# A fused attention and gated-MLP kernel on one Trainium2 core: the scores of attention tile 4 are written behind the outputs of tile 2 instead of in front of them

## The chip, the core and the metric

The kernel runs on one core of a Trainium2 chip. The core has a matrix engine (TensorE, PE in the profile, with its weight loads as PEld), a vector engine (VectorE, DVE), an activation engine (ScalarE, ACT), a general-purpose engine (GpSimd, POOL) and a synchronisation engine (SyncE, SP), which here issues all DMAs. Each engine works through its own list of instructions in order and waits for the others at semaphores. The metric is the time of one execution on the device, in microseconds (us).

## The reference

The program computes block attention over chunks of 64 tokens, and feeds the result into a gated MLP that also mixes along the sequence. Sizes: B = 8 batches, H = 8 heads, S = 576 tokens, D = 64 per head, so the model width is 512; d_ff = 1024.

```python
scores = scale * q_c @ k_c.T                 # per chunk of 64 tokens
attn   = softmax(scores)                     # minus the row maximum, / (sum + 1e-09)
x      = attn @ v_c                          # -> (B, S, 512)

h    = gelu_tanh(x @ w_in)                   # (B, S, 1024)
u, v = h[..., :512], h[..., 512:]
v_n  = (v - mean(v)) / sqrt(var(v) + 1e-06) * g_ln
v_s  = einsum('ts,bsd->btd', w_sg, v_n) + b_sg[None, :, None]
out  = x + (u * v_s) @ w_out
```

All inputs and outputs are float32; in memory w_in and w_out arrive as 8-byte words, which the kernel turns into float32 pairs itself.

## The kernel before, in words

**Tiles and units.** The 8 x 576 tokens make 36 attention tiles of 128 tokens (tile 4 has the last 64 tokens of batch 0 and the first 64 of batch 1). For each tile there are three steps: `S` (scores and softmax, `att_scores`), `T` (transpose of the probabilities, `att_transpose`) and `O` (outputs, `att_out`). An output tile is evacuated by `keep()` into three copies: `xh` (the high part, cast on ScalarE, L94), `xl` (the rest, subtracted on VectorE, L97) and `xf` (the full value, copied on ScalarE, L432). The MLP of a batch is made of units: five or four `v` units (x @ the v half of w_in for 128 tokens, gelu, layer norm), four `u` units (x @ a quarter of the u half, gelu), four `s` units (w_sg @ v_n, gate) and four `o` units (@ w_out, plus x, store). The name v02 is the unit v of batch 0, part 2; v04 is the fifth part, which takes the odd 64 tokens of batches 0 and 1 together. Products of high precision are made of three matmuls each (high x high, high x low, low x high).

**The weights.** w_in has to be split into a high and a low part. `W`/`w` do it for the v half (four pieces), `X`/`x` for the u half (four pieces): `X` (`pair_begin`, L130 on ScalarE, then L131, L132, L133, L162, L166 on VectorE) prepares the words in place, and `x` (`pair_end`) forms the high part on ScalarE (L174), sums four products on TensorE (L178) in a PSUM buffer, and evacuates the low part on ScalarE (L179). `G` issues the loads of w_sg (L235) and its bias, `g` splits one of its five pieces each (L94 or L250 on ScalarE, L97 or L251 on VectorE). `L` and `A` issue loads of w_in and of the attention inputs (L297, L301), `M` a small load, `D` some spare matmuls; `P`, `Q` are scores and outputs of two tiles at once, `Y` prepares w_out.

**A v unit.** Twelve matmuls (L452) into a PSUM buffer; gelu on ScalarE (L455, output `hs`); L458, L459, L460 on VectorE take mean and variance (`sm`); GpSimd raises the variance to the power -0.5 (L461); L467 on VectorE subtracts the mean and multiplies by g_ln; L469 on ScalarE and L470 on VectorE write the high and the low part. In v04, L474 and L475 on ScalarE (two each) and L476 on VectorE take the place of the last two, and write `z`. A u unit is 24 matmuls and one gelu on ScalarE (L496).

**Buffers.** There are three PSUM buffers `pm` in rotation: for scores, for L178's products, and for the v, u, s and o units. The next user of a buffer waits until the evacuation of the one before is done. The transposes and outputs of tiles 0 to 4 alternate between two halves of one PSUM tile, `banks`: the transposes of tile 3 write where O2's outputs stood, so they wait for xh, xl and xf of tile 2; likewise tile 4's for tile 3's.

**Softmax.** For tiles 0, 2 and 4 (`ACT_SOFTMAX`) the exponentials are taken head by head on ScalarE (L344, eight instructions per tile) straight from the scores; in the others VectorE subtracts the maximum first (L346) and ScalarE takes one exponential (L349).

**What sets the order.** For batches 0 and 1 the order of all steps is written out by hand in the string `START`, a letter and a number for each step; a loop calls the functions in this order. A layer below records the instructions and, when the program is built, sets their order on each engine from these calls and from what they depend on, so moving one step in `START` can move instructions of other steps too. From batch 2 on, a table of slots places the attention steps between the units.

The lines that carry the name of a step in `START`:

```python
for step in START.split():
    steps[step[0]](int(step[1:]))
```

Of the kernel before, what the change touches and what calls it, by code (L numbers as in the profile page):

```python
# [42 lines left out]


START = """
L0 A0 L1 A1 L2 L3 A4 W0 S0 W1 D8 w0 S1 W2 T0 w1 S2 O0 T1 W3 w2 S3 O1 T2 M0 w3 S4 O2 T3 v00 X0 O3 G0 T4 v01 x0 X1 O4 A8
v02 x1 X2 v03 X3 v04 u00 x2 g0 g1 u01 x3 g2 P5 g3 u02 g4 T5 u03 T6 s00 P7 Q5 s01 s02 T7 T8 s03 Q7 v10 v11 Y0 v12 Y1
v13 Y2 u10 Y3 u11 Y4 u12 Y5 Y6 u13 Y7 A10 s10 A12 s11 P9 s12 s13 T9 o00 T10 P11 o01 o02 o03 Q9 A14 T11 o10 T12 o11 Q11
S13 A15 o12 T13 o13
# [587 lines left out]
```

## Time and profile before

| what | value |
| --- | --- |
| time, median of 3 runs (lowest to highest) | 508.56 us (508.21 to 508.85) |
| the profiled execution: time; span of its instructions | 508.83 us; 507.0 us |
| mean granted TensorE clock in it | 0.998 |
| busy share of TensorE, VectorE, ScalarE, GpSimd | 97%, 67%, 54%, 14% |

The time of an execution is a little longer than the span from the first to the last recorded instruction (here by 1.83 us). The busy share says in how much of the span an engine worked; all times of instructions below are counted from the start of the span. A row of a timeline gives start, duration, engine, line of the program, operation, output and inputs, sizes, how many instructions the row groups, and in brackets the idle time before it and what ended it. A row of the chain of waits gives start, length, engine, what it wrote, line.

### The profile page before, as it was taken

How to read it: one execution, taken by the hardware profiler on the slowest of the kernel's cores; microseconds unless marked ns; L12 is line 12 of the kernel's file. 1: busy time of each engine (PE TensorE's matmuls, PEld its weight loads, DVE VectorE, ACT ScalarE, POOL GpSimd, SP SyncE). 2: the span in 40 equal slices, each digit the busy share in tenths (PEclk: the TensorE clock that was granted, in tenths of full speed). 3: DMA queues.
4: the chain of work that ended last, by engine and by line, in shares of the span. 5: the costliest groups of instructions: out<-in, count | busy, mean ns of one | idle time of the engine just before them, and what ended most of it. 6: DMA issues, size and time to landing. Idle time of an engine off the chain costs nothing.

```text
span 507.0 us, 12386 instructions
## 1 busy us (share of the span) xinstructions
PE 494.4 (97%) x5244; PEld 458.1 (90%) x5244; DVE 339.1 (67%) x707; ACT 274.7 (54%) x509; POOL 69.9 (14%) x72
## 2 busy tenths in 40 slices
PE   5999999999999999999999999999999999999996
PEld 4667898799999899989999899999999899999996
DVE  7998779888856947586563866576565676536141
ACT  5899667753445764355642775355643766334210
POOL 0112100210211401022100321022100141002000
PEclk9999999999999999999999999999999999999999
DMA  8948010228167204241324204060415200010002
GB/s 335 326 136 234 3 35 25 69 78 207 34 186 227 64 11 117 86 134 39 89 66 154 63 1 127 37 183 2 125 26 170 87 1 4 25 71 0 1 1 93
DMA packets 49595, 46.58 MB, mean 92 GB/s; under 512 B 35202, under 2 KB 39554, under 8 KB 49540
## 3 DMA queue, kind: packets, MB, share of 16 engines
q1 hardware_dynamic: 49540, 45.80, 30.3%
q8 instruction: 41, 0.67, 0.6%
q14 instruction: 14, 0.11, 0.1%
HBM read 36.34 MB, written 9.44 MB: 90 GB/s over the span
## 4 chain that ended last, share of the span: by engine, by line
PE 88%; DVE 6%; ACT 4%; DMA 1%; issue 1%; POOL 0%; DVEq 0%; SPq 0%; ACTq 0%
PE pm L509 21%; PE pm L489 20%; PE pm L532 19%; PE pm L452 18%; PE banks L322 3%; PE pm L410 3%; PE pm L178 2%; ACT pt L344 1%; DMA qkv_t<-qkv 1%; PE pm L314 1%; PE pm L577 1%; DVE gl L97 1%; DVE gt L513 1%; ACT L455 1%; DVE blocks L372 1%
## 5 line engine op out<-in xcount | busy, mean ns | idle before, releaser
L509 PE MATMUL pm<-wsg,v 128*128 128x288 f32 x768 | 107.9, 296 | 0.0
L509 PEld LDWEIGHTS pm<-wsg,v 128*128 128x128 f32 x768 | 103.9, 189 | 0.3
L532 PE MATMUL pm<-gh,wout 128*128 128x288 f32 x512 | 92.3, 297 | 0.0
L532 PEld LDWEIGHTS pm<-gh,wout 128*128 128x128 f32 x512 | 76.1, 189 | 0.5
L461 POOL TENSOR_TENSOR sm<-sm,neg_half 128x1 f32<-128x1 f32 x36 | 36.5, 1013 | 165.6 <-DVE sm L460 165.6
L358 POOL TENSOR_TENSOR pt<-pt,den 128x512 f32<-128x512 f32 x27 | 29.7, 1113 | 202.4 <-DVE den L357 128.0
L94 ACT CAST gh<-gt 128x576 fp32r<-128x576 f32 x32 | 21.5, 673 | 63.2 <-DVE gt L513 63.2
L532 PE MATMUL pm<-gl,wout 128*128 128x288 f32 x256 | 55.4, 296 | 0.0
L489 PE MATMUL pm<-xh,win_l 128*128 128x288 f32 x256 | 55.3, 298 | 0.0
L489 PE MATMUL pm<-xh,win_h 128*128 128x288 f32 x256 | 55.0, 296 | 0.0
L489 PE MATMUL pm<-xl,win_h 128*128 128x288 f32 x256 | 55.0, 296 | 0.0
L452 PE MATMUL pm<-win_h,xl 128*128 128x512 f32 x128 | 51.5, 402 | 1.4 <-DVE xl L97 0.9
L452 PE MATMUL pm<-win_l,xh 128*128 128x512 f32 x128 | 50.8, 397 | 0.0
L452 PE MATMUL pm<-win_h,xh 128*128 128x512 f32 x128 | 50.8, 396 | 0.0
L513 DVE TENSOR_TENSOR gt<-pm,u 128x576 f32<-128x576 f32 x32 | 24.1, 754 | 38.9 <-PE pm L509 38.9
L540 DVE TENSOR_TENSOR ot<-pm,xf 128x576 f32<-128x576 f32 (+1 forms) x33 | 24.1, 733 | 29.8 <-PE pm L532 29.7
L489 PEld LDWEIGHTS pm<-xh,win_l 128*128 128x128 f32 x256 | 41.4, 188 | 1.0
L532 PEld LDWEIGHTS pm<-gl,wout 128*128 128x128 f32 x256 | 41.4, 189 | 0.0
L489 PEld LDWEIGHTS pm<-xl,win_h 128*128 128x128 f32 x256 | 41.1, 188 | 0.0
L489 PEld LDWEIGHTS pm<-xh,win_h 128*128 128x128 f32 x256 | 41.0, 188 | 0.0
L97 DVE TENSOR_TENSOR xl<-pm,xh 128x512 fp32r<-128x512 f32 (+1 forms) x34 | 21.8, 641 | 26.2 <-ACT xh L94 26.2
L458 DVE BATCH_NORM_STATS2 sm<-hs 128x6 f32<-128x512 f32 x36 | 24.8, 689 | 20.9 <-ACT hs L455 20.7
(121 smaller groups left out, 820.0 us busy)
## 6 DMA issues: line engine op xcount, KB each, us to landing
qkv_t<-qkv SPq DMA_DIRECT2D x32, 512.0 KB, 4.6
out_dram<-ot SPq DMA_DIRECT2D x31, 288.0 KB, 2.2
qkv_t<-qkv SPq DMA_DIRECT2D x124, 64.0 KB, 3.7
qkv_t<-qkv SPq DMA_DIRECT2D x3, 768.0 KB, 11.9
wsg<-w_in SPq DMA_DIRECT2D x4, 512.0 KB, 6.1
wout<-w_in SPq DMA_DIRECT2D x4, 512.0 KB, 4.2
st<-w_out SPq DMA_DIRECT2D x8, 256.0 KB, 2.7
stage<-w_sg SPq DMA_DIRECT2D x5, 288.0 KB, 4.0
```

The costliest lines, as they stand in the source:

```text
L94: nc.scalar.copy(hi, src)
L97: lo_eng.tensor_tensor(lo, src, hi.bitcast(F32), op=ALU.subtract)
L322: nc.tensor.matmul(sc[o, c, h // 2, :], qt[r, 0, h, :], qt[r, 1, h, :], start=True, stop=True)
L358: (nc.gpsimd if t > last[1] else pick(f"n{t}")).tensor_tensor(pt, pt, den.unsqueeze(2).broadcast_to([P, H, D]), op=ALU.mult)
L452: nc.tensor.matmul(pv, a[:, kt, tok], c[:, kt, DH:], start=(i == 0), stop=(i == 11))
L458: nc.vector.bn_stats(st, h)
L461: nc.gpsimd.tensor_tensor(rs, rs, neg_half, op=ALU.pow)
L489: nc.tensor.matmul(pm[:, j, :HS], a[:, kt, dc], c[:, kt, j * HS : (j + 1) * HS], start=(i == 0), stop=(i == 11))
L509: nc.tensor.matmul(pm[:, j, :HS], a[:, dc], c[:, m, j * HS : (j + 1) * HS], start=(i == 0), stop=(i == len(ops) - 1))
L513: nc.vector.tensor_tensor(gt.rearrange("p (a c) -> p a c", a=2), pm[:, :, :HS], u2[0][:, dt, :].rearrange("p (a c) -> p a c", a=2), op=ALU ...
L532: nc.tensor.matmul(pm[:, j, :HS], a[:, kt, ec], c[:, kt, j * HS : (j + 1) * HS], start=(i == 0), stop=(i == len(ops) - 1),)
L540: nc.vector.tensor_tensor(ot[:, js], pm[:, js, :HS], res[:, js], op=ALU.add)
```

## The change

The step `S4` moves behind the step `O2` in `START`; nothing else is edited.

```diff
 START = """
-L0 A0 L1 A1 L2 L3 A4 W0 S0 W1 D8 w0 S1 W2 T0 w1 S2 O0 T1 W3 w2 S3 O1 T2 M0 w3 S4 O2 T3 v00 X0 O3 G0 T4 v01 x0 X1 O4 A8
+L0 A0 L1 A1 L2 L3 A4 W0 S0 W1 D8 w0 S1 W2 T0 w1 S2 O0 T1 W3 w2 S3 O1 T2 M0 w3 O2 S4 T3 v00 X0 O3 G0 T4 v01 x0 X1 O4 A8
 v02 x1 X2 v03 X3 v04 u00 x2 g0 g1 u01 x3 g2 P5 g3 u02 g4 T5 u03 T6 s00 P7 Q5 s01 s02 T7 T8 s03 Q7 v10 v11 Y0 v12 Y1
```

No instruction is added or removed (ScalarE's list shows 3 rows more, because rows that were grouped fall apart). The order of S4's and O2's own matmuls on TensorE stays as it is; what changes on the engines behind it is this.

ScalarE, from tile 4's exponentials on (`pt`, `den` with L344; `xh` and `xf` are those of tile 2, `hs<-pm` is gelu of v00, then of v01; `ptT` is of tile 3, `win_h<-wsg_186` is x0's high part):

```order
-L344 ACTIVATE pt,den<-pm,nmax 128x64 x8
+L344 ACTIVATE pt,den<-pm,nmax 128x64 x2
 L94 CAST xh<-banks 128x2x4x64
-L455 ACT_TABLE_LOAD
-L455 ACTIVATE hs<-pm 128x512
+L344 ACTIVATE pt,den<-pm,nmax 128x64 x5
 L432 COPY xf<-banks 128x2x4x64
+L344 ACTIVATE pt,den<-pm,nmax 128x64
+L455 ACT_TABLE_LOAD
+L455 ACTIVATE hs<-pm 128x512
+L368 COPY ptT<-banks 128x512
 L174 ACTIVATE win_h<-wsg_186 128x4x128
```

Tile 2's cast xh moved from behind the eighth exponential to behind the second, its copy xf from behind the gelu of v00 to ahead of it and of the table load.

VectorE, between v00's L467 and the subtraction xl of tile 3, before (`wsg_234` are the words of x1's quarter, the first `v` is v00's low part, the L458 is v01's):

```order
L467 SCALAR_TENSOR_TENSOR hs<-hs,sm,g_bc 128x512
L131 TENSOR_SCALAR wsg_234<-wsg_234 128x512
L132 TENSOR_SCALAR wsg_234<-wsg_234 128x512
L133 SCALAR_TENSOR_TENSOR wsg_234<-wsg_234 128x512
L470 SCALAR_TENSOR_TENSOR v<-hs,sm,v 128x512
L458 BN_STATS sm<-hs 128x6
L97 TENSOR_TENSOR xl<-banks,xh 128x2x4x64
```

The same place now:

```order
L467 SCALAR_TENSOR_TENSOR hs<-hs,sm,g_bc 128x512
L458 BN_STATS sm<-hs 128x6
L131 TENSOR_SCALAR wsg_234<-wsg_234 128x512
L459 BN_AGGR sm<-sm 128x2
L132 TENSOR_SCALAR wsg_234<-wsg_234 128x512
L470 SCALAR_TENSOR_TENSOR v<-hs,sm,v 128x512
L97 TENSOR_TENSOR xl<-banks,xh 128x2x4x64
```

v01's statistics moved ahead of v00's low part, L133 behind xl.

ScalarE, from the last L469 of batch 0's v units to the gelus of u00 and u01 (`u_705`), before (`L179` is x2's low part, `bh` belongs to the bias of w_sg, the `z` are v04's):

```order
L469 ACTIVATE v<-hs,sm 128x512
L496 ACTIVATE u_705<-pm 128x576
L255 CAST bh<-bt 1x576
L179 ACTIVATE win_l<-pm 128x4x128
L474 ACTIVATE z_0_94<-hs,sm 64x512
L474 ACTIVATE z_1_95<-hs,sm 64x512
L475 CAST z_0_96<-z_0_94 64x512
L475 CAST z_1_97<-z_1_95 64x512
L496 ACTIVATE u_705<-pm 128x576
```

The same place now:

```order
L469 ACTIVATE v<-hs,sm 128x512
L255 CAST bh<-bt 1x576
L474 ACTIVATE z_0_94<-hs,sm 64x512
L474 ACTIVATE z_1_95<-hs,sm 64x512
L475 CAST z_0_96<-z_0_94 64x512
L475 CAST z_1_97<-z_1_95 64x512
L496 ACTIVATE u_705<-pm 128x576
L179 ACTIVATE win_l<-pm 128x4x128
L496 ACTIVATE u_705<-pm 128x576
```

The gelu of u00 and x2's L179 moved from ahead of v04's four z instructions to behind them.

Elsewhere: on TensorE the transposes of tile 3 come after two of v01's matmuls instead of seven, and those of tile 4 after four of v02's instead of five. On VectorE, between v02's L470 and v04's L460, the L162 and L166 of x3's quarter (`wout_376`) are now inside, and one L97 of w_sg and the L251 are behind; v02's L467 is followed by L133 instead of L166. SP issues w_sg's four loads (L235) ahead of tile 6's load (L297) instead of behind it. GpSimd's order is the same.

## The prediction

> **What bounds the kernel now.** I read the page first (busy shares), then TensorE's waits, then the chain of work that ended last, then the timelines of the engines that the chain names. The page says that TensorE is the bound:
>
> ```profile
> span 507.0 us, 12386 instructions
> PE 494.4 (97%) x5244; PEld 458.1 (90%) x5244; DVE 339.1 (67%) x707; ACT 274.7 (54%) x509; POOL 69.9 (14%) x72
> ```
>
> So a change of order can only add or take away moments in which TensorE waits. Its waits from 43 us to the end (what waited, for whom; us in total, times, longest) leave little:
>
> ```profile
> PE pm L410 <- ACT ptT L380: 0.9, 1, 0.9
> PE pm L452 <- ACT hs L455: 0.3, 1, 0.3
> ```
>
> What the change touches lies before 60 us. There the chain (start, length, what) leaves TensorE and comes back to it at 38.35:
>
> ```profile
> 28.21 2.48 ACT pt L344 x16
> 30.69 0.48 ACT xh L94
> ...
> 31.19 1.28 ACT L455
> ...
> 32.48 0.61 ACT hs L455
> 33.11 0.70 DVE sm L458
> ...
> 35.71 0.69 DVE wsg L133
> 36.40 0.66 DVE v L470
> 37.06 0.60 DVE sm L458
> 37.67 0.64 DVE xl L97
> ...
> 38.35 1.43 PE pm L452 x5
> ```
>
> The reader is to see: tile 4's eight exponentials, the cast xh of tile 2's outputs behind them, the table load for gelu, gelu of v00, its statistics on VectorE, and xl of tile 3, for which v02 waits. TensorE's timeline shows both waits, at v01 (31.95) and at v02 (38.35), and the later place x3 (58.13):
>
> ```profile
> 30.67 0.40 PE L452 MATMUL pm<-win_h,xh 128*128 128x512 f32 x1
> 31.95 0.50 PE L452 MATMUL pm<-win_h,xl 128*128 128x512 f32 x1 [0.88 <-DVE xl L97]
> 32.29 0.40 PE L452 MATMUL pm<-win_l,xh 128*128 128x512 f32 x1
> ...
> 37.66 0.59 PE L178 MATMUL pm<-win_h,ident 128*128 128x512 f32 x1
> 38.35 0.50 PE L452 MATMUL pm<-win_h,xl 128*128 128x512 f32 x1
> ...
> 58.13 1.02 PE L178 MATMUL pm<-wout,ident 128*128 128x512 f32 x2
> ```
>
> **Part 1: the wait at v01 goes.** No instruction is added or removed. S4's and O2's matmuls keep their places on TensorE; what moves is the evacuation of O2 on ScalarE and VectorE. The rows for it:
>
> ```profile
> 30.55 0.63 ACT L94 CAST xh<-banks 128x512 fp32r<-128x512 f32 x1
> 32.98 0.58 ACT L432 COPY xf<-banks 128x512 f32<-128x512 f32 x1
> 33.44 0.65 ACT L174 ACTIVATE win_h<-wsg 128x512 fp32r<-128x512 f32 x1
> 29.00 0.69 DVE L133 SCALAR_TENSOR_TENSOR wsg<-wsg 128x512 int32<-128x512 int32 x1
> 29.73 0.43 DVE L162 TENSOR_SCALAR wsg<-wsg 128x512 int32<-128x512 int32 x1
> ```
>
> xh of tile 2 now follows the second exponential, so at about 28.8 (28.21 plus two eighths of 2.48) instead of 30.55; it ends at 29.4. xl then stands on VectorE behind L133, which ends at 29.7, and is done by about 30.3. TensorE can use it when v00's last matmul (30.67) has gone: matmuls of this shape go in every 0.23 us (an estimate from 1.43 us for x5 less the last one's 0.5), so v01's second matmul moves from 32.29 to about 31.13. Gain 1.16 us. If the order brought nothing it would be 0; it cannot be more, since TensorE has no further idle time here.
>
> **Part 2: most of it comes back at v02.** ScalarE now does the copy xf (33.44 − 32.98 = 0.46 of its queue) ahead of the table load, so gelu of v00 starts at about 32.93 instead of 32.48, and the statistics and POOL's power follow 0.45 later. On VectorE v01's L458 moves ahead of v00's L470, and L133 of x1's quarter moves behind. L470 comes at about 36.6 (before: 36.32, queue-bound), xl of tile 3 directly behind it at 37.26 (before 37.60, with L458 between), v02 at 38.0 instead of 38.35. So of 1.16 us, 0.34 is left at v02, and TensorE waits there for about 1 us. The transposes of tile 4 then wait for xf of tile 3 about as in the kernel before; I carry 0.3 us of gain from v02 on. Ends: 0 to 0.6, by 0.2 to 0.3 us of ScalarE drain around the table load either way.
>
> The DMAs: w_sg's four loads wait on SP for O3, now at 35.4 instead of 36.56, and go ahead of tile 6's first load, which has until 59.7. ScalarE now casts the first of them at 39.0, before the copy ptT of tile 4 that O4 waits for. The time to landing of the first two:
>
> ```profile
> DMA to landing us min/median/max: 2.9/3.6/4.3
> ```
>
> With 2.9 it has landed at 38.3 and costs nothing; with 4.3 at 39.7 it would hold O4 by 0.7 us. The queues are empty in front of it as in the kernel before, so I take 2.9.
>
> **Part 3: a new wait at x3.** x3's first product (58.13) needs the PSUM buffer of u00, which gelu of u00 frees. In the kernel before, that gelu stands on ScalarE ahead of v04's four z instructions; now it stands behind them:
>
> ```profile
> 54.08 0.65 ACT L496 ACTIVATE u<-pm 128x576 f32<-128x576 f32 x1 [0.19 <-DVE wsg L97]
> 56.57 1.47 ACT L474 ACTIVATE z<-hs,sm 64x512 fp32r<-64x512 f32 x2 [0.52 <-POOL sm L461]
> 58.06 1.26 ACT L475 CAST z<-z 64x512 fp32r<-64x512 f32 x2
> 59.22 0.64 ACT L496 ACTIVATE u<-pm 128x576 f32<-128x576 f32 x1
> ```
>
> From the first z to the instruction behind the four are 59.22 − 56.57 = 2.65 us, plus 0.65 for the gelu itself. So x3 starts 3.35 us after z does (0.05 for the semaphore), and z starts when POOL's power of v04 is done. How early is that now? The rows:
>
> ```profile
> 38.67 0.74 DVE L467 SCALAR_TENSOR_TENSOR hs<-hs,sm,g_bc 128x512 f32<-128x512 f32 x1
> 38.84 0.99 POOL L461 TENSOR_TENSOR sm<-sm,neg_half 128x1 f32<-128x1 f32 x1 [3.55 <-DVE sm L460]
> 39.33 0.68 DVE L166 SCALAR_TENSOR_TENSOR wsg<-wsg 128x512 uint16<-128x512 uint16 x1
> ...
> 46.04 0.74 DVE L467 SCALAR_TENSOR_TENSOR hs<-hs,sm,g_bc 128x512 f32<-128x512 f32 x1
> 46.27 2.19 POOL L461 TENSOR_TENSOR sm<-sm,neg_half 128x1 f32<-128x1 f32 x1 [0.95 <-DVE sm L460]
> 47.30 0.75 DVE L97 TENSOR_TENSOR wsg<-stage,wsg 128x576 fp32r<-128x576 f32 x1
> 49.26 0.75 DVE L470 SCALAR_TENSOR_TENSOR v<-hs,sm,v 128x512 fp32r<-128x512 f32 x1 [1.20 <-ACT v L469]
> 54.68 0.72 DVE L251 TENSOR_TENSOR wsg<-stage,wsg 64x576 fp32r<-64x576 f32 x1
> 55.33 0.14 DVE L460 TENSOR_SCALAR sm<-sm 128x1 f32<-128x1 f32 x1
> ...
> 103.67 2.00 POOL L461 TENSOR_TENSOR sm<-sm,neg_half 128x1 f32<-128x1 f32 x1 [2.15 <-DVE sm L460]
> ```
>
> The short power ends 0.41 after VectorE's L467 beside it (38.84 + 0.99 against 38.67 + 0.74); the long one, v02's, ends 0.41 after the L97 that follows two instructions later (46.27 + 2.19 against 47.30 + 0.75). v02: one L162 less (0.3) stands ahead of its L467, and the group starts 0.17 earlier, so that L97 ends at 47.58, the power at 47.99, and L470 of v02 starts at 48.75, 0.5 earlier. From there to v04's L460 took 6.07 us (55.33 − 49.26) without a gap worth counting. Now one L97 (0.66 of queue) and L251 (0.64) stand behind it, and L162 (0.34) and L166 (0.6) of x3's quarter ahead: 5.7, so L460 at 54.5 and L467 from 54.6 to 55.35. With a short power z starts at 55.8, 0.8 earlier than before. Then x3 starts at 55.8 + 3.35 = 59.15. Unheld it would have started at 58.13 − 0.3 = 57.8; it waits some 1.3 us. After a wait the next matmul is 0.1 late as well (31.95 to 32.29 is 0.34, not 0.23).
>
> **Sum.** 59.15 − 58.13 + 0.1 = +1.1 us. From x3 on TensorE has no wait that the change could shorten: P5, the u and s units keep their order and shift as one. The profiled execution took 508.83 us (span 507.0), 0.27 over the median of the runs, 508.56; I put the sum on the median: **509.6 us**, +0.2%. That is just about what a measurement of this kernel can tell from no change (0.2%, 1.02 us). The unknowns in it (drain at the table load, 0.05 to 0.1 us at each of three hand-overs) make it +0.7 to +1.5, so 509.2 to 510.1.
>
> **Rivals.**
> (a) *v02's power is not held.* The trace has both kinds: 0.99 at 38.84, 2.19 at 46.27, and 2.00 once more at 103.67. If v02's takes 0.99 us it ends 1.2 earlier; so does the queue behind it, z starts at 54.6, gelu of u00 is out at 57.9, and x3 is held by at most 0.1. Then the 0.3 us from v02 stay: 508.3 us, not slower. It decides at 57.8, when TensorE reaches x3. Against it: the pair behind v02's L467 is again two full-length instructions with two SBUF inputs (L133 in L166's place, then L97). Chance 0.14.
> (b) *v04's power is held too.* Behind v04's L467 there now stand L97 and L251 without a gap. If it ends 0.41 after L251 (56.58 by the queue), z starts 1.2 us later still and x3 with it: 510.9 us. Against it: at 38.84 the power got through although L166 followed directly; and v04's power, like that one, now waits for a single semaphore. Chance 0.12. [...]
> (c) *The first w_sg load lands late* (4.3 us): O4 0.7 later, v02's gelu and all of part 3 with it: 510.3 us. Chance 0.06.
> (d) *The 1.16 us are kept.* If xl of tile 3 came by 37.0, v02 would not wait, and gelu of u00 came out before x3: 507.2 us. That needs gelu of v00 no later than now, though xf is ahead of it. Chance 0.06.
> (e) *Nothing measurable* because the two parts cancel within 0.5 us: 508.6 us. Chance 0.06.
>
> **How the numbers follow.** The forecast case has 0.56; its 509.2 to 510.1 lies around the bound at 509.58, 0.3 above it and 0.26 below. Slower by over 0.2%: 0.3 + 0.12 + 0.06 = 0.48. Faster by over 0.2%: (d) and the far end of (a), 0.08. Within: the rest, 0.44. The range goes from (a) with 0.1 to spare to (b): 508.2 to 511.0; only (d) and the tails lie outside. The forecast's own range is 509.2 to 510.1.
>
> **What would show it.** Right: TensorE's wait at v01 is gone; v02 still waits for xl of tile 3 and starts 0.2 to 0.5 earlier than 38.35; x3's first L178 waits about 1.3 us for ScalarE's L496 of u00, at about 59.1; from there to the end the distances are those of before. v02's power lasts 2 us, v04's about 1. Wrong, if x3 shows no wait (then (a) or (d)), if z starts at 57 (then (b)), or if O4 waits for ptT (then (c)).

## The result, and the profile after

The changed kernel is slower: 513.06 us in the median of 5 runs (511.85 to 515.27) against 508.54 us (508.21 to 508.85, 5 runs); the ratio is 1.009, with a 95% interval of 1.0075 to 1.0104. (Of all executions below, two that were disturbed, of 690 and 1689 us, are left out.) The forecast was 509.6 us, slower, with a range up to 511.0: the sign was right, the size was not.

The profiled execution took 514.18 us. The head of its page:

```profile
span 512.4 us, 12378 instructions
PE 495.7 (97%) x5238; PEld 458.6 (90%) x5244; DVE 339.2 (66%) x707; ACT 274.4 (54%) x509; POOL 73.5 (14%) x72
```

TensorE is still the bound; GpSimd (POOL) is busy for 73.5 us instead of 69.9, with the same instructions. TensorE's waits (what waited, for whom; us in total, times, longest):

```profile
PE pm L178 <- ACT u L496: 3.0, 1, 3.0
PE banks L398 <- ACT ptT L368: 1.4, 2, 1.1
PE pm L452 <- DVE sm L460: 0.9, 1, 0.9
```

The first is x3, the longer of the second two is at tile 4's outputs O4, the third is v02. (The view names L460 for v02 because it ended last, at 37.87; the instruction that v02 needs, xl of tile 3, ended just ahead of it, at 37.81.) TensorE's timeline at the same places (v01, v02, O4, x3's three rows, and P5 behind it):

```profile
30.69 0.40 PE L452 MATMUL pm<-win_h,xl 128*128 128x512 f32 x1
...
37.86 0.50 PE L452 MATMUL pm<-win_h,xl 128*128 128x512 f32 x1 [0.87 <-DVE sm L460]
...
41.82 1.15 PE L398 MATMUL banks<-ptT,qkv_t 64*64 64x64 f32 x32 [1.06 <-ACT ptT L368]
...
61.90 2.08 PE L178 MATMUL pm<-wout,ident 128*128 128x512 f32 x2 [2.99 <-ACT u L496]
63.77 1.06 PE L178 MATMUL pm<-wout,low 128*128 128x512 bf16 x2
64.27 0.83 PE L178 MATMUL pm<-win_h,ident 128*128 128x512 f32 x1
65.03 1.16 PE L322 MATMUL banks<-qkv_t 64*64 64x64 f32 x64
```

P5 in the kernel before:

```profile
59.76 1.16 PE L322 MATMUL banks<-qkv_t 64*64 64x64 f32 x64
```

The wait at v01 is gone, as forecast, and x3 waits for the gelu of u00, as forecast, but for 2.99 us instead of 1.3. Two things are new: O4 waits 1.06 us, and x3's own matmuls take twice as long. TensorE's stretches of 1 us there (length, busy time and number of matmuls, granted clock, share and rate of the DMAs) say why:

```profile
61.00:62.00 1.00, 0.10 (x1) 0.69 0.00 0
62.00:63.00 1.00, 1.00 (x2) 0.50 0.00 0
63.00:64.00 1.00, 1.00 (x3) 0.50 0.00 0
64.00:65.00 1.00, 1.00 (x3) 0.60 0.00 0
65.00:66.00 1.00, 1.00 (x65) 1.00 0.00 0
```

The granted clock falls to 0.50 still within the wait, at about 61.4, and is back at 1.0 at about 64.8 (estimates from the means 0.69 and 0.60): some 3.4 us. Now the 5.4 us that the span grew (512.4 − 507.0) can be laid out: x3 starts at 61.90 instead of 58.13, 3.77 later; from x3 to P5 it takes 65.03 − 61.90 = 3.13 instead of 59.76 − 58.13 = 1.63 in the kernel before, 1.50 more; the other 0.1 is spread over the 447 us behind. The 3.77 are 0.78 by which TensorE is done later with what stands ahead of x3 (58.91) and the 2.99 of the wait.

Who was late? The rows of GpSimd's powers (v01, v02, v03, v04), for v01, v03 and v04 with the VectorE instruction that ended last before the power did, and what waited for them on ScalarE and VectorE:

```profile
37.94 2.60 POOL L461 TENSOR_TENSOR sm<-sm,neg_half 128x1 f32<-128x1 f32 x1 [2.38 <-DVE sm L460]
39.71 0.42 DVE L132 TENSOR_SCALAR wout<-wout 128x512 int32<-128x512 int32 x1
40.58 0.72 ACT L469 ACTIVATE v<-hs,sm 128x512 fp32r<-128x512 f32 x1 [1.14 <-POOL sm L461]
41.20 0.57 ACT L368 COPY ptT<-banks 128x512 f32<-128x512 f32 x1
...
46.65 2.20 POOL L461 TENSOR_TENSOR sm<-sm,neg_half 128x1 f32<-128x1 f32 x1 [0.71 <-DVE sm L460]
49.64 0.75 DVE L470 SCALAR_TENSOR_TENSOR v<-hs,sm,v 128x512 fp32r<-128x512 f32 x1 [1.20 <-ACT v L469]
...
52.19 1.59 POOL L461 TENSOR_TENSOR sm<-sm,neg_half 128x1 f32<-128x1 f32 x1 [3.35 <-DVE sm L460]
52.69 0.68 DVE L166 SCALAR_TENSOR_TENSOR wout<-wout 128x512 uint16<-128x512 uint16 x1
54.57 0.75 DVE L470 SCALAR_TENSOR_TENSOR v<-hs,sm,v 128x512 fp32r<-128x512 f32 x1 [0.59 <-ACT v L469]
55.98 0.15 DVE L460 TENSOR_SCALAR sm<-sm 128x1 f32<-128x1 f32 x1
56.20 2.32 POOL L461 TENSOR_TENSOR sm<-sm,neg_half 128x1 f32<-128x1 f32 x1 [2.42 <-DVE sm L460]
57.37 0.74 DVE L251 TENSOR_TENSOR wsg<-stage,wsg 64x576 fp32r<-64x576 f32 x1
58.56 1.47 ACT L474 ACTIVATE z<-hs,sm 64x512 fp32r<-64x512 f32 x2 [2.53 <-POOL sm L461]
61.21 0.64 ACT L496 ACTIVATE u<-pm 128x576 f32<-128x576 f32 x1
```

In the kernel before, v01's power took 0.99 us and v02's 2.19; v03's and v04's there:

```profile
52.15 0.99 POOL L461 TENSOR_TENSOR sm<-sm,neg_half 128x1 f32<-128x1 f32 x1 [3.69 <-DVE sm L460]
55.61 0.93 POOL L461 TENSOR_TENSOR sm<-sm,neg_half 128x1 f32<-128x1 f32 x1 [2.47 <-DVE sm L460]
```

Those three short ones ended 0.41 or 0.42 us behind their own unit's L467. Now v01's, v03's and v04's end 0.41 us behind a VectorE instruction four, one and two places behind that L467: 40.54 behind 40.13 (L132), 53.78 behind 53.37 (L166), 58.52 behind 58.11 (L251). For v01's, ScalarE waits with L469, the copy ptT of tile 4 stands behind it, and O4 waits for that. For v04's, ScalarE waits with z, the gelu of u00 stands behind, and x3 waits for that.

### The profile page after: what moved, and what is told of

Read it like the earlier page. It is cut to its first block, busy times and chain, and to the rows that moved or that the text cites. A ratio compares the mean times of both kernels' runs of the same rounds, so it can differ in the third digit from the quotient of the medians.

```text
span 512.4 us, 12378 instructions
## 1 busy us (share of the span) xinstructions
PE 495.7 (97%) x5238; PEld 458.6 (90%) x5244; DVE 339.2 (66%) x707; ACT 274.4 (54%) x509; POOL 73.5 (14%) x72
## 4 chain that ended last, share of the span: by engine, by line
PE 83%; DVE 7%; ACT 5%; POOL 2%; issue 1%; DMA 1%; DVEq 0%; SPq 0%; ACTq 0%; POOLq 0%
PE pm L509 21%; PE pm L532 19%; PE pm L489 19%; PE pm L452 16%; PE banks L322 3%; PE pm L410 3%; POOL sm L461 2%; PE pm L178 1%; ACT pt L344 1%; DMA qkv_t<-qkv 1%; PE pm L314 1%; PE pm L577 1%; DVE gl L97 1%; DVE gt L513 1%; DVE pt L358 1%
## 5 line engine op out<-in xcount | busy, mean ns | idle before, releaser
L461 POOL TENSOR_TENSOR sm<-sm,neg_half 128x1 f32<-128x1 f32 x36 | 40.1, 1114 | 167.4 <-DVE sm L460 167.3
L97 DVE TENSOR_TENSOR xl<-pm,xh 128x512 fp32r<-128x512 f32 (+1 forms) x34 | 21.8, 640 | 26.3 <-ACT xh L94 26.3
L458 DVE BATCH_NORM_STATS2 sm<-hs 128x6 f32<-128x512 f32 x36 | 24.8, 688 | 21.0 <-ACT hs L455 20.8
## 6 DMA issues: line engine op xcount, KB each, us to landing
qkv_t<-qkv SPq DMA_DIRECT2D x32, 512.0 KB, 5.0
wsg<-w_in SPq DMA_DIRECT2D x4, 512.0 KB, 6.0
wout<-w_in SPq DMA_DIRECT2D x4, 512.0 KB, 4.0
```

Source lines behind the costliest of these rows:

```text
L97: lo_eng.tensor_tensor(lo, src, hi.bitcast(F32), op=ALU.subtract)
L458: nc.vector.bn_stats(st, h)
L461: nc.gpsimd.tensor_tensor(rs, rs, neg_half, op=ALU.pow)
```

## The experiments

Each kernel was timed against the kernel before, run beside it; that one had medians of 508.9 to 509.2 us there (508.1 to 510.7). Times below are medians.

**v01's power taken away.** The first three experiments take a power off GpSimd without moving any other instruction. They leave out the power itself: a multiplication on VectorE stands in its place, so the scale of these units is not computed. The unit is (0, 1) here, (0, 4) in the second, both in the third:

```diff
-        nc.gpsimd.tensor_tensor(rs, rs, neg_half, op=ALU.pow)
+        (nc.vector if (b, m) in ((0, 1),) else nc.gpsimd).tensor_tensor(
+            rs, rs, neg_half, op=ALU.mult if (b, m) in ((0, 1),) else ALU.pow)
```

> The changed kernel, with the power of v01 alone (2.60 us on GpSimd in its trace) replaced by one multiplication of the same 128x1 on VectorE (about 0.15 us), so that v01's scale is wrong and nothing else moves on any engine. Theory: GpSimd is held by VectorE's back-to-back instructions, ScalarE waits for it with v01's L469, and the copy ptT of tile 4 behind it makes O4 wait 1.06 us. Then L469 starts at about 39.4 instead of 40.58, O4's wait falls to 0.1 or less, and all before x3 comes 1.0 us earlier; x3 keeps a wait of about 3 us: 512.0 us against 513.1. Rival: ptT is held by the cast of w_sg's first piece ahead of it in ScalarE's queue, then O4 still waits 0.5 us or more and the time is 512.6 to 513.1.

Measured: 512.64 us (6 runs), ratio 1.0071 (1.0055 to 1.0086). TensorE's waits:

```profile
PE pm L178 <- ACT u L496: 2.9, 1, 2.9
PE banks L398 <- ACT ptT L368: 0.4, 1, 0.4
```

O4's wait of 1.06 is gone from the trace (the 0.4 left is the one of another tile, which the kernel before has too), so ptT was held by L469 and L469 by the power; the cast of w_sg in the queue was not the cause. The time does not show it: 512.0 was expected, 512.64 lies where the rival was put, and a gain of about 1 us is inside the spread of the changed kernel.

**v04's power taken away.**

> The changed kernel, with the power of v04 alone (2.32 us on GpSimd) replaced by one multiplication on VectorE, v04's scale being wrong; no other instruction moves. Theory: z starts right behind v04's L467, at about 57.0 instead of 58.56, gelu of u00 ends 1.6 us earlier, and x3 waits 1.4 us instead of 2.99. If the half clock seen behind the wait comes from its length it goes as well (another 1.6 us): 509.9 us; if the clock drops behind a wait of 1.4 us too: 511.4 us. Rival: gelu of u00 waits for something other than the z instructions; then the time stays at 513.

Measured: 511.52 us (5 runs), ratio 1.0049 (1.0036 to 1.0062). The wait at x3, and v01's power, which is on GpSimd here as in the changed kernel:

```profile
PE pm L178 <- ACT u L496: 1.3, 1, 1.3
38.00 0.99 POOL L461 TENSOR_TENSOR sm<-sm,neg_half 128x1 f32<-128x1 f32 x1 [2.38 <-DVE sm L460]
```

x3's wait fell by 1.7 us, as expected, and the clock stayed at 1.0. The second row was not expected: v01's power is short in this execution, with the same instructions around it. The time missed its 509.9: this execution took 509.89 us and was the fastest of the five, the other four took 511.5 to 511.8, also with a mean clock of 0.999 or 1.0. So it was not the clock; that v01's power was long in those four (it costs 1.06 us in the trace of the changed kernel) would fit, but they left no trace.

**Both taken away.**

> Both powers replaced by multiplications on VectorE (v01's and v04's scales wrong), no other instruction moved. This is the prediction's forecast case: no wait at O4, x3 waits about 1.3 us for gelu of u00, no lasting clock drop. 509.6 us by its sum (509.2 to 510.1). If both terms are as large as the trace says the difference to the changed kernel is 1.0 + 1.6 us + the clock's part. Rival: with v01's wait gone, everything on VectorE and GpSimd moves 1 us with TensorE and x3 waits as in the run with v04's power alone; the two still add. If it comes out below 508.8, the long powers were the whole of the loss.

Measured: 510.04 us (12 runs), ratio 1.0015 (1.0005 to 1.0025), that is 0.83 us slower than the kernel before beside it (0.25 to 1.3 by the interval). The wait at O4 is gone; v02's 0.9 is as in the changed kernel, and at x3 there is this:

```profile
PE pm L178 <- ACT u L496: 1.3, 1, 1.3
```

This is close to the kernel that the prediction described, and its +1.1 us was about right for it, in part because two things offset each other: v03's power is long here too (1.59 us, for which VectorE stands idle for 0.60 us ahead of L470), and v04's z waits for no power at all. The two long powers, and what hangs on them, are most of the rest.

**One more instruction on VectorE.** A BN_STATS behind v04's L467, which the build puts behind the L97 that follows; L251, which stood there, goes behind L476:

```diff
         nc.vector.scalar_tensor_tensor(h, h, mv[:, 0:1], g_bc, op0=ALU.subtract, op1=ALU.mult)
+        if (b, m) in ((0, 4),):
+            nc.vector.bn_stats(pause, h[:, :512])
```

> The changed kernel with one more instruction on VectorE: a BN_STATS of 128x512 (0.69 us, result unused) that comes to stand between the L97 and the L251 behind v04's L467; L251 goes behind v04's L476. GpSimd keeps its power. Theory (a GpSimd power is held while VectorE's two-input instructions follow each other, and gets through at a BN_STATS): v04's power ends 0.41 us behind that L97, at 57.9 instead of 58.5, and x3 comes 0.65 us earlier although VectorE has more work: 512.4 us, less by up to 1.6 if the clock does not drop. Rival (the power is long by itself or by chance): power 2.3 us as before, time 513 us. Second rival (any VectorE instruction holds it): the power lasts until 0.41 behind BN_STATS, 2.3 us, 513 us.

Measured: 511.53 us (11 runs), ratio 1.0045 (1.0024 to 1.0065). VectorE, GpSimd and the wait (line numbers are one to three higher here):

```profile
56.54 0.75 DVE L97 TENSOR_TENSOR wsg<-stage,wsg 128x576 fp32r<-128x576 f32 x1
57.21 0.69 DVE L470 BATCH_NORM_STATS2 pause<-hs 128x6 f32<-128x512 f32 x1
56.04 1.66 POOL L462 TENSOR_TENSOR sm<-sm,neg_half 128x1 f32<-128x1 f32 x1 [2.42 <-DVE sm L461]
PE pm L179 <- ACT u L499: 2.4, 1, 2.4
```

The power ends at 57.70, 0.41 behind the end of L97 (57.29), while BN_STATS is running: it is held by L97 and not by BN_STATS. More work on VectorE made the wait shorter, by 0.6 us (2.38 instead of 2.99; 0.65 was expected). The clock fell here too (a mean of 0.73 from 60 to 62 us, 0.50 from 62 to 64, 0.92 from 64 to 66), with a wait of 2.38 us.

**Spare work in the gap.** Twelve spare matmuls into the PSUM tile `banks`:

```diff
-... u01 x3 g2 ...
+... u01 F12 x3 g2 ...
+    def fill(n):
+        for _ in range(n):
+            nc.tensor.matmul(banks[:, 0, :P], ident, ident, start=True, stop=True)
```

> The changed kernel with twelve spare matmuls (128x128 float32, into the PSUM tile of the early transposes, which nobody uses then) on TensorE between u01 and x3; nothing else moves. Theory: the granted clock of 0.50 from 62 to 65 us in the changed kernel's trace follows from TensorE standing idle for 2.99 us, and costs 1.6 us more than the wait itself. With some 2.5 us of spare work in the gap the clock stays at 1.0 and x3's matmuls take 1.02 us instead of 2.08, while x3 starts as late as before: 511.5 us against 513.1. Rival: the clock falls for another reason (the load of all engines at that place); then 513 or, where x3 would have been ready earlier, more.

> The kernel with twelve spare matmuls between u01 and x3 once more, because its profiled execution was a disturbed one. Theory (the clock falls because TensorE stands idle): the clock between 58 and 66 us stays at 1.0, x3's first row of two matmuls takes 1.0 to 1.1 us instead of 2.08, and x3's start does not move: 1.6 us less than the changed kernel run beside it. Rival (the clock falls by itself there): the same clock of 0.5, no gain.

Measured: 511.29 us (5 runs) the first time, without a trace of one of these, and 512.01 us (6 runs) the second, ratio 1.0052 in both (1.0033 to 1.0071, and 1.0040 to 1.0064). The second trace:

```profile
58.97 2.84 PE L584 MATMUL banks<-ident 128*128 128x128 f32 x24
61.65 1.02 PE L178 MATMUL pm<-wout,ident 128*128 128x512 f32 x2
```

The clock stays at 1.0 from 60 to 68 us, and x3's first row takes 1.02 instead of 2.08. None of the eleven executions with spare work has a mean clock below 0.998, against 8 of 13 of the changed kernel (counted below); one trace alone could not show it, as the next run tells. The expected gain of 1.6 us over the changed kernel beside it came out as 0.8 in the medians (512.84 to 512.01), with intervals that overlap: the changed kernel itself does not always lose the clock. Also v02's power was short in this execution, the gelu was done at 60.87, and the spare work itself then cost 0.8.

**The changed kernel again.**

> The changed kernel as it is, for a second trace and for times beside those of the next run on the same chip. If v01's power is held by chance, it takes 0.99 or 2.60 us here, and O4 waits 0.4 or less in the first case and about 1.1 in the second; v02's, v03's and v04's powers take 2.2, 1.6 and 2.3 us as in the first trace; x3 waits 3.0 us, with the clock at 0.50 behind it: 511.5 to 514, 513 in the median. Rival: the long powers of the first trace were one bad execution; then several of them take 0.99 us here and x3's wait is 1.5 us or less.

Measured: 512.84 us (8 runs, 510.13 to 515.52), ratio 1.0074 (1.0048 to 1.0100). Its trace:

```profile
61.82 1.13 PE L178 MATMUL pm<-wout,ident 128*128 128x512 f32 x2 [2.97 <-ACT u L496]
37.86 2.60 POOL L461 TENSOR_TENSOR sm<-sm,neg_half 128x1 f32<-128x1 f32 x1 [2.38 <-DVE sm L460]
```

The same waits to 0.02 us, and yet no fall of the clock: x3's row takes 1.13. So the long powers are not one bad execution, and of the two traces of this kernel one has the fall of the clock at the wait (2.99 us) and one has not (2.97 us). By arithmetic, an estimate, a clock of 0.5 for 3.4 of 512 us makes the mean of an execution 0.997, and for twice that time 0.993. Over both sets the changed kernel ran 13 times: 8 had a mean clock of 0.997 or less (two of them 0.993) and a median of 513.7 us, 5 had 0.999 or more and 511.85 us. The half clock is worth 1.9 us by these, 1.5 us by the rows above.

**The gelu of u00 ahead of the casts.** v04's last four instructions on ScalarE become a step of their own, `z`, written behind u00 (the lines that make it a step are left out here):

```diff
-... v04 u00 x2 ...
+... v04 u00 z0 x2 ...
```

> The changed kernel with v04's z part written behind u00: on ScalarE gelu of u00 (L496 of the changed kernel) stands ahead of the two casts z (1.26 us) and still behind the two L474; no other engine's order changes. Theory: x3 waits for that gelu alone, so its wait falls by 1.26 to about 1.7 us, and if the clock needs a longer wait than that to fall, by 1.6 more: 510.2 us; if it falls all the same, 511.8. Rival: the casts only swap places with the wait (TensorE waits for z elsewhere, at s00): 513.

Measured: 510.84 us (9 runs), ratio 1.0031 (1.0016 to 1.0045), all with a clock of 0.999 or 1.0. ScalarE and x3's wait (L483 is the first z, L505 the gelu):

```profile
56.78 1.46 ACT L483 ACTIVATE z<-hs,sm 64x512 fp32r<-64x512 f32 x2 [2.53 <-POOL sm L461]
58.27 0.65 ACT L505 ACTIVATE u<-pm 128x576 f32<-128x576 f32 x1
58.97 1.12 PE L178 MATMUL pm<-wout,ident 128*128 128x512 f32 x2 [1.75 <-ACT u L505]
```

The wait fell by the 1.26 us of the two casts, to 1.75, and TensorE has no new wait elsewhere in this trace. ScalarE's queue is what x3 waits for.

**The whole repair, in three steps.** With `z0` as above, x3 behind P5, and short pauses (BN_STATS of 128x64) behind the L467 of v04; then also of v01; then also of v02:

```diff
-... u01 x3 g2 P5 g3 u02 ...
+... u01 g2 P5 x3 g3 u02 ...
+        if (b, m) in ((0, 1), (0, 2), (0, 4)):
+            nc.vector.bn_stats(pause, h[:, :64])
```

> As the run before, and also x3 behind the scores P5 (1.1 us of TensorE work that needs no gelu), and a short BN_STATS (128x64) on VectorE behind the L97 that follows v04's L467. All outputs as in the reference. Theory: each of the three takes a piece of x3's wait (1.26, 1.1, and up to 0.66 if the short pause is enough for GpSimd to get through): nothing is left of 2.99 us, no clock drop; O4's wait of 1.06 us stays in the executions in which v01's power is held. 508.5 us where it is not held, 509.6 where it is. Rival: x2's and x3's low parts or the exponentials behind P5 come late on ScalarE and u02 or u03 waits for them: 510 or more.

> As the run before, with a second short BN_STATS behind the L133 that follows v01's L467 (some instructions of VectorE behind it change places). Theory: v01's power gets through there, at 39.5 at the latest instead of 40.5, O4 waits 0.1 us or less in nearly every execution, and what is left of the change is its gain of 0.3 us at v02: 0.3 us less than the kernel before, and a narrow spread (under 1 us). Rival: the short pause (some 0.15 us) is not enough for GpSimd, v01's power takes 2 us or more in some executions, and the spread stays at 2 us.

> The changed kernel with v04's z part behind u00, x3 behind P5, and short BN_STATS behind v01's, v02's and v04's L467. With these, gelu of u00 stands on ScalarE ahead of all four z instructions, as in the kernel before. Theory: x3 does not wait at all, whatever the powers take; O4 waits 0.2 us or less; v02 waits 0.9 us as in every run of the changed order, where the kernel before waits 0.9 at v01: the change itself is worth 0.3 us or nothing, 508.3 to 509.2 us, no slower than the kernel before (ratio 0.998 to 1.000). Rival: the order S4 behind O2 has a cost of its own that none of these takes away; then 510 or more.

Measured: 509.09 us (508.23 to 510.86), ratio 1.0005 (0.9993 to 1.0018); 509.01 us (507.56 to 509.77), ratio 0.9995 (0.9984 to 1.0006); 508.15 us (507.37 to 508.99), ratio 0.9981 (0.9971 to 0.9991); 12 runs each. The first lies between the two times expected for it, 508.5 and 509.6. The second missed: neither the gain of 0.3 us nor a spread under 1 us came. Its spread is 2.2 us, as its rival said, though v01's power got through at the pause in its trace, and O4 hardly waited:

```profile
38.68 1.68 POOL L462 TENSOR_TENSOR sm<-sm,neg_half 128x1 f32<-128x1 f32 x1 [2.38 <-DVE sm L461]
41.64 1.15 PE L399 MATMUL banks<-ptT,qkv_t 64*64 64x64 f32 x32 [0.15 <-ACT ptT L369]
```

In the third, the gelu of u00 (L508) stands ahead of all four z (L486 is the first), as in the kernel before, and x3 does not wait, though v04's power still takes 1.65 us:

```profile
54.94 0.65 ACT L508 ACTIVATE u<-pm 128x576 f32<-128x576 f32 x1
56.68 1.47 ACT L486 ACTIVATE z<-hs,sm 64x512 fp32r<-64x512 f32 x2 [0.59 <-POOL sm L462]
59.49 1.13 PE L179 MATMUL pm<-wout,ident 128*128 128x512 f32 x2
PE pm L453 <- DVE sm L461: 0.9, 1, 0.9
PE banks L399 <- ACT ptT L369: 0.4, 1, 0.4
```

So S4 behind O2 has no cost that these edits do not take away: with the gelu ahead of z again, x3 behind P5 and the powers let through earlier, the changed order is 0.19% faster than the kernel before, with a spread of 1.6 us. How much of this is the change and how much the other edits is not told apart, since the kernel before can be helped by a pause too:

**A pause in the kernel before.** One BN_STATS of 128x64 behind v01's L467, nothing else in the source:

> The kernel before, with one short BN_STATS (128x64) behind the L166 that follows v01's L467, and what the build makes of it (x2's and x3's word steps on VectorE change places, v02's L469 comes earlier on ScalarE). Theory: the kernel before has the same draw at v01's power (0.99 us in its trace; its runs so far lie between 508.1 and 510.7), and a long one costs it O4's wait of 1 us too. Then a pause makes the runs narrower, about 508.2 to 509.2, with a median 0.4 us below that of the kernel before run beside it. Rival: its spread comes from elsewhere (the first loads, the stores); then spread and median stay.

Measured: 508.34 us (11 runs, 507.39 to 509.43), ratio 0.9986 (0.9974 to 0.9998). The median fell by 0.8 us, but the spread is 2.0 us as against 2.5 us beside it, and the build also moved some instructions of x2's and x3's words and v02's L469. So the gain is shown for the kernel as built; that it comes from v01's power is not. In both of this kernel's traces, before and with the pause, v01's power took 0.99 us.

## Why the prediction was wrong, point by point

- **Part 1, right.** v01's second matmul was to move from 32.29 to 31.13, a gain of 1.16. It is at 30.92, with v00's last matmul 0.22 earlier by itself: 1.15.
- **Part 2, right at v02, wrong at O4.** v02 was forecast at 38.0 and is at 37.86, waiting 0.87 where about 1 was said. (In the kernel before, the row at 38.35 shows no such wait: the matmul ahead of it ends at 38.25.) The drain of 0.2 to 0.3 us around the table load, in the range there and in that of the sum, was an estimate worked out from no row: the load starts 0.02 us behind the end of ScalarE's instruction ahead of it (31.47 behind 31.45; 0.01 in the kernel before), and gelu of v00 is at 32.76 instead of 32.93. But "I carry 0.3 us of gain from v02 on" failed at O4: the step left v01's power out, that is, took it at its 0.99 us of the kernel before without asking whether it could be held, though the instruction behind its L467 had changed from L166 to L133. It took 2.60 us in both traces and O4 gave back 1.06. That O4 waits for ptT was named as the sign of rival (c); the sign came, but not (c): the first w_sg cast started at 38.76 without a wait.
- **Part 3, right in mechanism, wrong in its main term.** That x3 waits for the gelu of u00 behind four z instructions, and starts 3.35 us after the first z, is what the trace shows: 61.90 − 58.56 = 3.34. The term "z at 55.8" was mis-sized by 2.76 us. v04's L460 came at 55.98 instead of 54.5: 0.89 of it was there already at v02's L470 (49.64 instead of 48.75), from v01's power, and 0.59 came from v03's power (1.59 us, for which VectorE stood idle ahead of v03's L470). The remaining 1.28 is v04's own power, which ended 0.41 behind L251 instead of behind L467 and took 2.32 us instead of 0.93. The prediction allowed for one held power, v02's, and that one came as said (2.20 us).
- **Rival (b) was the likeliest case, not one in eight.** It said that L97 and L251 without a gap would hold v04's power until 0.41 behind L251, and it did so, with 2.32 us, in every trace of this order without a pause in which the power is on GpSimd. Against it the prediction set the one short power at 38.84, a single row; the row at 46.27 was as good. That v04's power waits for a single semaphore, the other reason against it, did not help. The price of 510.9 us lacked v01's and v03's powers and the clock.
- **The clock was not in the sum at all.** No wait in the kernel before is longer than 1 us behind the start, so no row showed what comes behind a wait of 2 to 3 us; the half clock, where it came, cost 1.5 us by the rows of the profiled execution and 1.9 us by the medians of the 13. In the profiled execution the forecast's 1.1, the 2.75 by which x3 starts later than forecast and the clock's 1.5 make 5.35 of the 5.4 us.
- **The sum for the forecast case holds roughly.** With both powers taken away the kernel is 0.83 us slower than the one beside it, against +1.1 forecast, with v03's power still long in it and v04's costing nothing. (508.56 and 1.1 make 509.7, not 509.6; this changes nothing above.)

## What to carry to other kernels

An instruction is not short because one row says so (v01's power took 0.99 us in one trace and 2.60 us in another): where the instructions beside it on another engine change, price it also as held until the first gap in that engine's queue (v04's power took 2.32 us so), and follow what stands behind the waiting instruction in order. When a step is moved in a list, look past the two steps at every place where the build has changed the order of an engine that frees a buffer; here ScalarE's order 25 us later cost more than the 1.16 us that the move could bring. And a new wait on the engine that bounds the kernel can cost more than its length: the 2.99 us at x3 were followed by 1.50 us more.

## What the runs showed of the hardware

**GpSimd behind VectorE.** In the traces of the kernel before and of the changed kernel a 128x1 power on GpSimd takes 0.90 to 0.99 us where it ends 0.40 to 0.42 us behind the end of its own unit's L467 (once in each trace behind an L470 instead: 0.94 us at 97.31 before, 0.95 us at 102.41 now). It takes 1.59 to 2.60 us where VectorE's instructions follow each other without a gap and it ends 0.41 or 0.42 us behind a later one: 1.59 behind an L166, 2.00 behind an L133, 2.19 and 2.20 behind an L97, 2.32 behind L251, 2.60 behind L132. Two inputs are not needed for this: the one of 2.60 us ran past the ends of L133 (two inputs, 0.69 us) and of L131 and L162 (one input, 0.42 us each) until behind L132 (one input, 0.42 us). With a BN_STATS between L97 and L251, v04's power took 1.66 us instead of 2.32: so with one of 128x512, during which it ended, and with one of 128x64 in the first two steps of the repair, where the build has L251 directly behind it. With the same instructions around it a power is short in one execution and long in another: v01's took 2.60 us in the two traces of the changed kernel and 0.99 us in that with v04's power taken away and in that with the gelu ahead of the casts; v02's took 2.20 us in the changed kernel and 0.92 us in the second trace with spare work. What decides it stays open.

**The clock behind a wait.** In the four sets of runs whose trace has a wait of 2.38 to 2.99 us at x3, 17 of 30 executions had a mean clock of 0.997 or less; in the nine other sets none of 84. Three of the four traces show the fall itself: with 2.99 us in the changed kernel (0.69, 0.50, 0.50, 0.60 in stretches of 1 us from 61 on), with 2.9 us with v01's power taken away (0.59, 0.55 in stretches of 2 us from 60 on), and with 2.38 us with the BN_STATS (0.73, 0.50, 0.92, as above). In the fourth a wait of 2.97 us left the clock at 1.0. In each of the three the half clock lasted some 3.4 us, an estimate from these means, and for most of that time TensorE was at work again (in the changed kernel from 61.90 to about 64.8). A fall with 2.38 us and none with 2.97 us: the length of the wait alone does not decide it, and what does is not shown.
